# Two token tiles through TensorE's transpose and two through a transposing load, eight W1 units on the first two, an early table load and new issue orders

## The chip, the cores and the metric

The kernel runs on one core of a Trainium2 chip. The metric is device time in microseconds (us) of one execution, as the median of several runs. Profiles come from one execution of their own, and their times count from its first instruction. PE is TensorE, PEld its weight loads, DVE VectorE, ACT ScalarE, POOL GpSimd and SP SyncE; ACTq and SPq are the instruction queues of ACT and SP, which also issue DMAs.

## What is computed

A gated sum of two branches over one input x of 2048 tokens by 512, all bfloat16:

```python
def _A_ref(x, wqkv, w_phi, wo):
    qkv = (x @ wqkv).reshape(B, S, 3, H, Dh).transpose(2, 0, 3, 1, 4)
    q, k, v = qkv[0], qkv[1], qkv[2]
    pq = jnp.einsum("bhsd,hdf->bhsf", q, w_phi)
    pk = jnp.einsum("bhsd,hdf->bhsf", k, w_phi)
    phi_q = jnp.concatenate([_softmax(pq), _softmax(-pq)], axis=-1)
    phi_k = jnp.concatenate([_softmax(pk), _softmax(-pk)], axis=-1)
    kv = jnp.einsum("bhsf,bhsd->bhfd", phi_k, v)
    z  = jnp.einsum("bhsf->bhf", phi_k)
    num = jnp.einsum("bhqf,bhfd->bhqd", phi_q, kv)
    den = jnp.einsum("bhqf,bhf->bhq", phi_q, z)[..., None] + 1e-6
    return (num / den).transpose(0, 2, 1, 3).reshape(B, S, D) @ wo

def _B_ref(x, w1, w2):
    return jnp.maximum(x @ w1, 0) @ w2

g = _sigmoid((x * gate_w).sum(-1, keepdims=True))
return g * _A_ref(x, A_wqkv, A_w_phi, A_wo) + (1 - g) * _B_ref(x, B_w1, B_w2)
```

There are 32 heads of 16, D is 512 and the hidden width of branch B is 1376. Only A_x is read; B_x is not used.

## The kernel before

The kernel is a graph of 622 named tasks. Each has an engine, a function that issues its instructions, and the tasks it depends on. The dictionary ORDER at the top of the file lists, for each of the five engines, the tasks in the order in which that engine issues them; nothing is planned at run time. Waits on semaphores are derived from the dependencies, so an engine stands still at a task until what it depends on is done, and everything behind it in the same list stands too. The `dur`, `lat` and `boost` values in the code belong to the tool that made the lists and have no effect on the chip.

**Tiling.** The tokens are 4 chunks of 512, each of 4 tiles of 128. XT holds x transposed (four row blocks of 128, called j, by tokens), HT the hidden layer, transposed too. PS is the eight banks of PSUM, 512 float32 columns each.

**Names.** A unit `h{chunk}_{k}` is one block of 128 hidden columns (k from 0 to 10) for one chunk: four matmuls of 512 columns, one for each j (`pe_h`, L425), followed by a relu `rl{chunk}_{k}` (L503) into HT. The units 0 to 9 of a chunk use banks 3, 4 and 5 in turn. `f1_{j}` (L408) folds w_phi into the transposed key weights wkT, and `fe1_{j}` evicts the result (L376 on ACT, L378 on DVE). `pr_{k|q}{n}` is the projection of two tiles (L545), `ev_` its eviction (L577), `mx_`/`mn_` the maxima and minima on DVE, `t1_`/`t2_` the subtractions on POOL (L590), `ex_` the exponential on ACT, `sm_`/`rc_` sums and reciprocals on DVE, `nm_` the normalization on POOL (L604, L627). `v{m}` and `ve{m}` are the value projection and its eviction, `kv{m}` (L611) adds a tile to the state. After the last one, `nd{m}` (L654) applies the state to the queries, whose features a transposing DMA `tq{m}` has turned, `o{m}` divides, `to{m}` turns the result, `b{m}` (L676) is the second layer of branch B, `a{m}` (L682) the output projection in the same bank, `oe{m}` (L730) the gated eviction, and `st{m}` the store (L735). The last tile, 15, is cut in two column parts, `a15_0`, `oe15_0`, `st15_0` (ACT's queue, L722) and `a15_1`, `oe15_1`, `st15_1` (SP's queue).

**The first chunk.** x arrives untransposed for its four tiles (`x00` to `x03`, 128 KB each, L306, into spare space of FT), and PE turns each tile by matmuls with an identity (`xt{m}{n}`, L384: two blocks of 128 columns each); `xe{m}{n}` evicts into XT (n 0 on ACT, L396, n 1 on DVE, L399). The other three chunks come by transposing DMAs `x1` to `x3` (L311). W1's columns 0 to 511 come in four row blocks `w1a0` to `w1a3`; columns 512 to 1023 as one load `w1b`, the rest as `w1c`. Units 0 to 3 of chunk 0 are computed piecewise as data comes: `hh00`, `hh01` and `hh1` to `hh4` (`pe_h_first`, L439) take one row block of W1 at a time for all four units on the first 256 tokens, `hr0`, `hr1` units 0 and 1 on the third tile, and `h0_0` to `h0_3` what is left (`pe_h_rest`, L445). Units 4 and up are whole.

At the very start six matmuls on a constant (`warm0`, L292) keep PE busy until x00 is there. The ACT table is loaded by an instruction that the compiler puts in front of the first activation, `xe00`.

These are the heads of the lists around the change, and the end of ACT's:

```python
"sp":  x00 w1a0 w1a2 x02 x03 w1b wphi wkT w1c wv x1 x2 wqT x3 gw w2a w2b wo ...
"act": x01 w1a1 w1a3 xe00 xe10 xe20 xe30 rl0_0 rl0_1 rl0_3 rl0_2 rl0_4 fe1_1 fe1_3 rl0_5 ev_k0 ...
       ... oe10 st9 st10 oe11 st8 st11 oe12 st12 oe13 st13 oe15_0 st15_0
"pe":  warm0 xt00 xt01 xt10 xt11 hh00 hh01 hh1 hh2 xt20 xt21 hh3 xt30 xt31 hh4 hr0 hr1 h0_0 h0_1 h0_2 h0_3
       h0_4 h0_5 f1_0 f1_1 f1_2 f1_3 h0_6 pr_k0a pr_k0 h0_7 h0_8 pr_k1 h0_9 h1_0 ...
```

`x1` waits for `w1c` to have landed; the kernel's last instructions, on SP, wait for all stores.

Of the kernel before, what the change touches and what calls it, by code (L numbers as in the profile page):

```python
# [5 lines left out]
ACT = mybir.ActivationFunctionType  # L6
# [12 lines left out]
        "x00 w1a0 w1a2 x02 x03 w1b wphi wkT w1c wv x1 x2 wqT x3 gw w2a w2b wo hx0 hx1 hx2 tq0 tq1 "  # L19
        "hx3 to0 tq2 tq3 to1 tq4 tq5 to2 to3 tq6 to4 tq7 to5 tq8 to6 tq9 to7 tq10 tq11 to8 to9 tq12 "  # L20
        "to10 tq13 tq14 to11 tq15 to12 to13 to14 to15 st14 st15_1 "
    ),
    "pool": (
        "iota_r iota_i iota_c ones hpad t1_k0 t2_k0 t1_k1 t2_k1 t2_k2 t1_k2 t1_k3 t2_k3 nm_k0 nm_k1 t1_k5 t1_k4 t2_k4 "
        "nm_k2 nm_k3 t1_k6 t1_k7 t2_k7 t2_k5 nm_k4 t1_k8 t2_k6 t2_k8 nm_k5 t2_q0 t1_q0 nm_k6 t2_q1 t1_q1 nm_k7 "
        "ra_q0 nm_q0 nm_k8 t2_q2 t1_q2 ra_q1 nm_q1 t1_q3 t2_q3 ra_q2 nm_q2 t1_q4 t2_q4 ra_q3 nm_q3 t1_q5 t2_q5 "
        "ra_q4 nm_q4 t2_q6 t1_q6 ra_q5 nm_q5 t2_q7 t1_q7 t2_q8 t1_q8 ra_q6 nm_q6 ra_q7 nm_q7 ra_q8 nm_q8 "
    ),
    "act": (
        "x01 w1a1 w1a3 xe00 xe10 xe20 xe30 rl0_0 rl0_1 rl0_3 rl0_2 rl0_4 fe1_1 fe1_3 rl0_5 ev_k0 rl0_8 rl0_6 "  # L30
        "rl0_7 ev_k1 rl1_0 rl0_9 ev_k2 rl1_1 ex_k0 ev_k3 rl1_3 rl1_2 ve0 rl1_5 ex_k1 rl1_4 ve1 ev_k4 rl1_6 rl1_7 "
        "ex_k3 rl1_8 ev_k5 ex_k2 ve2 rl0_10 rl1_9 ev_k6 rl1_10 ve3 rl2_0 rl2_1 ve4 ex_k4 rl2_2 ev_k7 rl2_3 rl2_4 "
        "ve5 rl2_6 rl2_5 rl2_7 ve6 rl2_8 rl2_9 rl2_10 ve7 ex_k5 ev_k8 ge1 ve8 ge0 ex_k7 rl3_0 rl3_1 ve9 ev_q0 "
        "ex_k6 ve10 gp0 ev_q1 rl3_3 ex_k8 gp1 rl3_2 rl3_4 ve11 ev_q2 ex_q0 rl3_5 ve12 ev_q3 ve13 rl3_6 ve14 ev_q4 "
        "rl3_7 ex_q1 rl3_8 ve15 rl3_9 rl3_10 ex_q2 ev_q5 ex_q3 ev_q6 oe0 ev_q7 ex_q4 oe1 st1 oe2 st0 ex_q5 "
        "ge3 ev_q8 oe3 oe4 st3 oe5 ge2 st2 ex_q6 gp2 oe6 ex_q7 st5 st4 ex_q8 st6 oe7 oe8 gp3 oe9 st7 oe10 st9 st10 "
        "oe11 st8 st11 oe12 st12 oe13 st13 oe15_0 st15_0 "
    ),
    "dve": (
        "ident shift xe01 xe11 xe21 xe31 blk row4 wbd1 wbd3 mk wbd2 wbd0 fe1_0 fe1_2 mx_k0 mn_k0 mx_k1 mn_k1 "  # L40
        "mn_k2 mx_k2 mx_k3 mn_k3 sm_k0 rc_k0 sm_k1 rc_k1 mn_k4 mx_k4 mx_k5 sm_k2 gr0 rc_k2 gr1 mx_k6 sm_k3 rc_k3 "
        "mn_k7 sm_k4 mx_k7 rc_k4 mn_k5 gr2 fe0_0 fe0_1 fe0_2 fe0_3 mn_k6 mx_k8 mn_k8 sm_k5 rc_k5 mn_q0 mx_q0 "
        "sm_k6 rc_k6 sm_k8 go1 go0 sm_k7 mn_q1 mx_q1 rc_k7 sm_q0 mx_q2 rc_q0 rc_k8 mx_q3 mn_q3 mn_q2 mx_q4 sm_q1 "
        "kn1 kn0 kz0 kz1 rc_q1 mn_q4 gr3 rd0_1 rd0_0 o0_0 o0_1 sm_q2 rd1_0 rd1_1 rc_q2 mx_q5 o1_1 o1_0 mn_q5 "
        "rd2_0 rd2_1 o2_0 o2_1 sm_q3 rd3_1 rd3_0 rc_q3 o3_1 o3_0 mn_q6 rd4_1 o4_1 rd4_0 o4_0 sm_q4 rd5_0 rd5_1 "
        "rc_q4 o5_0 o5_1 mx_q6 rd6_1 rd6_0 o6_1 o6_0 sm_q5 rd7_1 rc_q5 o7_1 rd7_0 mx_q7 o7_0 mx_q8 mn_q8 mn_q7 "
        "rd8_0 rd8_1 o8_0 o8_1 sm_q6 rd9_1 rd9_0 rc_q6 o9_0 o9_1 rd10_1 rd10_0 o10_0 sm_q7 go2 o10_1 sm_q8 rd11_1 "
        "rd11_0 o11_0 rc_q8 o11_1 rc_q7 rd12_0 rd12_1 o12_1 o12_0 rd13_0 go3 rd13_1 o13_1 o13_0 rd14_0 rd14_1 "
        "o14_0 o14_1 rd15_0 rd15_1 o15_0 o15_1 oe14 oe15_1 "
    ),  # L50
    "pe": (
        "warm0 xt00 xt01 xt10 xt11 hh00 hh01 hh1 hh2 xt20 xt21 hh3 xt30 xt31 hh4 hr0 hr1 h0_0 h0_1 h0_2 h0_3 h0_4 "
        "h0_5 f1_0 f1_1 f1_2 f1_3 h0_6 pr_k0a pr_k0 h0_7 h0_8 pr_k1 h0_9 h1_0 pr_k2 h1_1 h1_2 pr_k3 h1_3 v0 h1_4 h1_5 v1 "
        "h1_6 pr_k4 h1_7 h1_8 v2 pr_k5 h1_9 kv0 h0_10 kv1 pr_k6 h1_10 v3 kv2 h2_0 h2_1 kv3 v4 pr_k7 h2_2 v5 h2_3 "
        "h2_4 h2_5 h2_6 h2_7 v6 h2_8 h2_9 h2_10 kv4 kv5 f0_0 kv6 f0_1 v7 f0_2 pr_k8 f0_3 h3_0 kv7 h3_1 v8 pr_q0 "
        "v9 h3_2 h3_3 v10 kv8 pr_q1 kv9 h3_4 v11 kv10 pr_q2 h3_5 kv11 v12 pr_q3 h3_6 v13 kv12 h3_7 v14 kv13 pr_q4 "
        "h3_8 h3_9 v15 kv14 h3_10 pr_q5 kv15 b0 nd0_0 nd0_1 b3 nd1_0 nd1_1 b2 pr_q6 a0 nd2_0 nd2_1 b1 nd3_1 pr_q7 "
        "nd3_0 b4 nd4_1 nd4_0 a1 pr_q8 nd5_1 a2 nd5_0 b5 a3 nd6_0 nd6_1 b6 nd7_0 nd7_1 a4 a5 b7 nd8_1 nd8_0 a6 b9 "
        "nd9_0 nd9_1 b8 nd10_0 nd10_1 a7 b10 nd11_1 a8 nd11_0 a9 b11 a10 nd12_0 nd12_1 b13 nd13_1 nd13_0 b12 "
        "nd14_0 nd14_1 b14 nd15_0 nd15_1 a11 a12 a13 b15_0 a14 a15_0 b15_1 a15_1 "  # L60
# [122 lines left out]
def bass_gated_mix__linear_kernel_hedgehog__dense_activation_relu__prompt_kernel(  # L183
# [38 lines left out]
    with ExitStack() as es:  # L222
# [101 lines left out]
        def load_w(j, eng, lat):  # L324
            load(f"w1a{j}", eng, W1[:, j, 0:512], w1r[:, j, 0:512], dur=0.45, lat=lat)
# [3 lines left out]
        load_w(0, "sp", 3.2)  # L329
        load_w(1, "act", 3.4)  # L330
        load_w(2, "sp", 3.8)
        load_w(3, "act", 3.95)
        load_x(2, "sp", 4.0)
        load_x(3, "sp", 3.9)
        load("w1b", "sp", W1[:, :, 512:1024], w1r[:, :, 512:1024], dur=0.5, lat=5.0)
        load("wphi", "sp", WPS[:, :, :], A_w_phi.rearrange("(g hl) r c -> (hl r) g c", g=ND), dur=0.5, lat=4.9)
        load_t("wkT", WT[:, ND:2 * ND, :], A_wqkv[:, D:2 * D], (), 4.1, 2.7)
# [42 lines left out]
        XB, FB = ((0, 1), (6, 7), (0, 1), (6, 7)), (0, 1, 6, 7)  # L380
# [7 lines left out]
        for m in range(4):  # L388
            for n in range(2):
                add(f"xt{m}{n}", "pe", lambda q, m=m, n=n: pe_xt(q, m, n),  # L390
                    (f"x0{m}", "ident", f"xe{m - 2}{n}" if m > 1 else None), dur=0.2, boost=9000.0 - 10 * m)
            for n, eng in enumerate(("act", "dve")):
                xo = XT[:, 2 * n:2 * n + 2, m * P:(m + 1) * P]
                xi = PS[:, XB[m][n], 0:2 * P].rearrange("p (j t) -> p j t", j=2)
                if eng == "act":
                    add(f"xe{m}{n}", eng, lambda q, o=xo, i=xi: q.activation(o, i, ACT.Copy), (f"xt{m}{n}",), dur=0.35,  # L396
                        boost=9000.0 - 10 * m)
                else:
                    add(f"xe{m}{n}", eng, lambda q, o=xo, i=xi: q.tensor_copy(o, i), (f"xt{m}{n}",), dur=0.37,  # L399
                        boost=9000.0 - 10 * m)  # L400
        x0 = [f"xe{m}{n}" for m in range(4) for n in range(2)]
# [11 lines left out]
        for c in range(NC):  # L413
            units += [("h", c, k) for k in range(KT - 1)]
# [5 lines left out]
        freed[FB[2]] = ("xe30",)  # L420
        w1of = {k: (() if k < 4 else ("w1b",) if k < 8 else ("w1c",)) for k in range(KT)}
# [15 lines left out]
        def pe_h_first(q, j, c0, c1, ks=range(4)):  # L437
            for k in ks:
                last = q.matmul(PS[:, GB4[k], c0:c1], W1[:, j, k * P:(k + 1) * P], XT[:, j, c0:c1],  # L439
# [3 lines left out]
        def pe_h_rest(q, k, c0, c1, first):  # L443
            for j in range(ND):
                last = q.matmul(PS[:, GB4[k], c0:c1], W1[:, j, k * P:(k + 1) * P], XT[:, j, c0:c1],  # L445
                                start=(j == 0 and first), stop=(j == ND - 1), skip_group_check=True)
            return last


        GB4 = (*HB, 2)  # L450
# [3 lines left out]
        for n, (j, ks) in enumerate(((1, range(4)), (2, range(4)), (3, (0, 1)), (3, (2, 3)))):  # L454
            add(f"hh{n + 1}", "pe", lambda q, j=j, ks=ks: pe_h_first(q, j, 0, 2 * P, ks),
                (f"xe0{j // 2}", f"xe1{j // 2}", f"w1a{j}", prev), dur=0.11 * len(ks), boost=8500.0)
            prev = f"hh{n + 1}"

        for k in range(2):
            add(f"hr{k}", "pe", lambda q, k=k: pe_h_rest(q, k, 2 * P, 3 * P, True), ("xe20", "xe21", prev), dur=0.22,  # L460
                boost=8200.0)
            prev = f"hr{k}"
        for line in (("warm0", "xt00", "xt01", "xt10", "xt11", "hh00", "hh01", "hh1", "hh2", "xt20", "xt21", "hh3", "xt30", "xt31",
                      "hh4", "hr0", "hr1"), ("xe00", "xe10", "xe20", "xe30"),
                     ("ident", "shift", "xe01", "xe11", "xe21", "xe31", "blk", "row4", "mk")):
# [10 lines left out]
        for n, (kind, a, k) in enumerate(units):  # L476
            b = GB4[n] if n < 4 else FB[2] if n == 4 else HB[(n - 4) % len(HB)]
            if kind == "h":
                halved = n < 4
                deps = [*xof[a], *w1of[k], prev, *freed[b]]  # L480
                if k == KT - 1:
# [17 lines left out]
                    pe_h_rest(q, k, (3 if k < 2 else 2) * P, 4 * P, k > 1) if h else pe_h(q, a, k, b),  # L499
                    deps, dur=(0.22 if k < 2 else 0.44) if halved else 0.87,  # L500
# [279 lines left out]
```

## Time and profile before

| | us |
|---|---|
| median of 3 runs | 150.24 (150.15 to 150.57) |
| the profiled execution | 149.87 |
| its span, first to last instruction | 148.3 |
| PE busy | 145.5 |
| DVE busy | 111.7 |
| POOL busy | 109.6 |
| ACT busy | 91.4 |

An engine's busy time is the sum of the stretches in which it executes; matmuls overlap each other, since the next starts before the one ahead has left the array. A line of the chain or of the timeline gives the start, the length, the engine (and in the chain what it writes), the line of the code and the number of instructions merged; brackets give the idle time ahead and what ended it. The first microseconds of the other engines, from the timeline:

```profile
3.99 0.81 ACT L396 ACTIVATE XT<-PS 128x256 bf16<-128x256 f32 x2 [0.56 <-PE PS L384]
4.20 0.85 DVE L399 CAST XT<-PS 128x256 bf16<-128x256 f32 x2 [1.84 <-PE PS L384]
...
6.55 0.82 ACT L396 ACTIVATE XT<-PS 128x256 bf16<-128x256 f32 x2 [1.75 <-PE PS L384]
...
6.67 0.87 DVE L399 CAST XT<-PS 128x256 bf16<-128x256 f32 x2 [1.61 <-PE PS L384]
```

### The profile page before, as it was taken

How to read it: one execution, taken by the hardware profiler on the slowest of the kernel's cores; microseconds unless marked ns; L12 is line 12 of the kernel's file. 1: busy time of each engine (PE TensorE's matmuls, PEld its weight loads, DVE VectorE, ACT ScalarE, POOL GpSimd, SP SyncE). 2: the span in 40 equal slices, each digit the busy share in tenths (PEclk: the TensorE clock that was granted, in tenths of full speed). 3: DMA queues.
4: the chain of work that ended last, by engine and by line, in shares of the span. 5: the costliest groups of instructions: out<-in, count | busy, mean ns of one | idle time of the engine just before them, and what ended most of it. 6: DMA issues, size and time to landing. Idle time of an engine off the chain costs nothing.

```text
span 148.3 us, 2542 instructions
## 1 busy us (share of the span) xinstructions
PE 145.5 (98%) x1009; PEld 75.3 (51%) x1009; DVE 111.7 (75%) x169; ACT 91.4 (62%) x126; POOL 109.6 (74%) x72
## 2 busy tenths in 40 slices
PE   7999999999999999999999999999999999999994
PEld 2875444445654475445444545455444444445453
DVE  2433666998896948989999997999999988634502
ACT  3475769799969765898983937175583751310141
POOL 4000499999999999999999999999999793150000
PEclk9999999999999999999999999999999999999999
DMA  4998999910040001000000093646957785556752
GB/s 139 324 256 220 169 187 214 340 51 4 0 73 0 0 4 38 0 0 4 0 0 0 7 141 71 141 95 138 183 119 167 180 214 116 141 134 158 64 157 92
DMA packets 46363, 16.11 MB, mean 109 GB/s; under 512 B 39856, under 2 KB 46352, under 8 KB 46352
## 3 DMA queue, kind: packets, MB, share of 16 engines
q1 hardware_dynamic: 43760, 13.61, 42.6%
q10 hardware_dynamic: 2592, 2.34, 4.9%
q8 instruction: 8, 0.13, 0.4%
q14 instruction: 3, 0.02, 0.1%
HBM read 4.41 MB, written 2.10 MB: 44 GB/s over the span
## 4 chain that ended last, share of the span: by engine, by line
PE 98%; DVE 0%; issue 0%
PE PS L676 24%; PE PS L425 21%; PE PS L545 19%; PE PS L526 9%; PE PS L682 9%; PE PS L611 3%; PE PS L654 3%; PE PS L433 2%; PE PS L292 2%; PE PS L698 2%; PE PS L439 2%; PE PS L445 1%; PE PS L408 1%; PE PS L384 1%; PE PS L709 1%; DVE OSB L719 0%
## 5 line engine op out<-in xcount | busy, mean ns | idle before, releaser
L590 POOL TENSOR_TENSOR TS<-PB,MX 128x1024 bf16<-128x1024 bf16 (+1 forms) x18 | 30.9, 1723 | 14.5 <-DVE MX L581 14.5
L676 PE MATMUL PS<-W,HT 128*128 128x512 bf16 (+1 forms) x165 | 38.1, 379 | 0.0
L597 DVE TENSOR_REDUCE ZB<-FT 128x128 f32<-128x2048 bf16 (+1 forms) x18 | 36.6, 2031 | 1.8 <-ACT FT L595 1.8
L595 ACT ACTIVATE FT<-TS 128x2048 bf16<-128x2048 bf16 (+1 forms) x18 | 30.9, 1718 | 9.6 <-POOL TS L590 9.5
L425 PE MATMUL PS<-XT,W 128*128 128x512 bf16 x144 | 34.7, 379 | 0.0
L590 POOL TENSOR_TENSOR TS<-MN,PB 128x1024 bf16<-128x1024 bf16 (+1 forms) x18 | 30.9, 1726 | 0.8 <-DVE MN L583 0.8
L545 PE MATMUL PS<-WP,XT 128*128 128x512 bf16 x128 | 30.6, 379 | 0.0
L604 POOL TENSOR_TENSOR FT<-FT,SC 128x2048 bf16<-128x2048 bf16 (+1 forms) x9 | 29.6, 3293 | 0.0
L503 ACT ACTIVATE HT<-PS 128x512 bf16<-128x512 f32 x40 | 22.6, 597 | 5.4 <-PE PS L425 4.6
L581 DVE TENSOR_REDUCE MX<-PB 128x64 bf16<-128x1024 bf16 (+1 forms) x18 | 19.5, 1085 | 5.9 <-ACT PB L577 5.9
L676 PEld LDWEIGHTS PS<-W,HT 128*128 128x128 bf16 (+1 forms) x165 | 15.4, 98 | 16.9
L730 ACT ACTIVATE OSB<-PS,OMG 128x512 bf16<-128x512 f32 x14 | 9.6, 686 | 21.1 <-PE PS L682 20.5
L583 DVE TENSOR_REDUCE MN<-PB 128x64 bf16<-128x1024 bf16 (+1 forms) x18 | 19.3, 1084 | 3.2 <-ACT PB L577 3.2
L425 PEld LDWEIGHTS PS<-XT,W 128*128 128x128 bf16 x144 | 13.7, 98 | 15.4
L577 ACT ACTIVATE PB<-PS 128x1024 bf16<-128x1024 f32 (+1 forms) x18 | 16.7, 927 | 7.2 <-PE PS L545 4.0
L545 PEld LDWEIGHTS PS<-WP,XT 128*128 128x128 bf16 x128 | 12.1, 98 | 13.5
L526 PE MATMUL PS<-WV,XT 128*128 128x512 bf16 x64 | 16.4, 379 | 0.0
L627 POOL TENSOR_TENSOR FT<-FT,SR 128x1024 bf16<-128x1024 bf16 (+1 forms) x9 | 15.7, 1740 | 0.7
L682 PE MATMUL PS<-WO,OT 128*128 128x512 bf16 x60 | 14.9, 378 | 0.0
L663 DVE SCALAR_TENSOR_TENSOR OTM<-PS,EG,RD 128x256 bf16<-128x256 f32 x32 | 13.8, 463 | 0.2
L661 DVE RECIPROCAL RD<-PS 128x16 f32<-128x16 f32 x32 | 6.4, 232 | 9.0 <-PE PS L654 8.8
L535 ACT ACTIVATE VS<-PS 128x512 bf16<-128x512 f32 x16 | 9.6, 602 | 4.3 <-PE PS L526 4.3
(55 smaller groups left out, 106.6 us busy)
## 6 DMA issues: line engine op xcount, KB each, us to landing
out_dram<-OSB ACTq DMA_DIRECT2D x14, 128.0 KB, 2.2
W<-in_B_w_dram SPq DMA_DIRECT2D x1, 1280.0 KB, 7.5
W<-in_B_w_dram SPq DMA_DIRECT2D x1, 512.0 KB, 4.5
WV<-in_A_wqkv_dram SPq DMA_DIRECT2D x1, 512.0 KB, 4.9
WO<-in_A_wo_dram SPq DMA_DIRECT2D x1, 512.0 KB, 7.5
FT<-in_A_x_dram SPq DMA_DIRECT2D x3, 128.0 KB, 3.1
W<-in_B_w_dram SPq DMA_DIRECT2D x1, 352.0 KB, 4.1
W<-in_B_w_dram ACTq DMA_DIRECT2D x2, 128.0 KB, 3.3
```

What stands on the lines that cost most here:

```text
L425: last = q.matmul(PS[:, b, :], W1[:, j, k * P:(k + 1) * P], XT[:, j, chunk(c)], start=(j == 0), stop=(j == ND - 1))
L503: add(f"rl{a}_{k}", "act", lambda q, a=a, k=k, b=b: q.activation(HT[:, k, chunk(a)], PS[:, b, :], ACT.Relu), (prev,), dur=0.6, boost=RL)
L526: last = q.matmul(PS[:, 2, :], XT[:, j, m * P:(m + 1) * P], WV[:, j, :], start=(j == 0), stop=(j == ND - 1))
L545: last = q.matmul(PS[:, n, :], XT[:, j, m * P:(m + 1) * P], WP[:, s, j, :], start=(j == 0), stop=(j == ND - 1))
L581: add(f"mx_{J}", "dve", lambda q, sl=sl, w=w, i=pbg: q.tensor_reduce(MX[:, sl, 0:w * H], i, AX.X, ALU.max), (f"ev_{J}", old("t1")), dur=0. ...
L583: add(f"mn_{J}", "dve", lambda q, sl=sl, w=w, i=pbg: q.tensor_reduce(MN[:, sl, 0:w * H], i, AX.X, ALU.min), (f"ev_{J}", old("t2")), dur=0. ...
L590: add(f"{tn}_{J}", "pool", lambda q, o3=o3, a3=a3, b3=b3: q.tensor_tensor(o3, a3, b3, ALU.subtract), (f"{'mx' if sg == 0 else 'mn'}_{J}", ...
L595: add(f"ex_{J}", "act", lambda q, fs=fs, ts=ts, w=w: q.activation(FT[:, fs, 0:w * F], TS[:, ts, 0:w * F], ACT.Exp), (f"t1_{J}", f"t2_{J}", ...
L597: add(f"sm_{J}", "dve", lambda q, fs=fs, sl=sl, w=w: q.tensor_reduce(ZB[:, sl, 0:2 * w * H], FT[:, fs, 0:w * F].rearrange("p (g d) -> p g ...
L604: add(f"nm_{J}", "pool", lambda q, f3=f3, sl=sl, w=w: q.tensor_tensor(f3, f3, SC[:, sl, 0:2 * w * H].unsqueeze(2).to_broadcast([P, 2 * w * ...
L676: last = q.matmul(PS[:, ab, :], HT[0:r, k, m * P:(m + 1) * P], W2[0:r, k, :], start=(k == 0), stop=False)
L682: last = q.matmul(PS[:, ab, :], OT[:, m % NOT, t, :], WO[:, t, :], start=False, stop=(t == ND - 1))
```

## The change

Tiles 2 and 3 of the first chunk no longer go through PE: `x02`, `x03`, `xt20` to `xt31` and `xe20` to `xe31` are gone, and one transposing DMA `x0b` writes their part of XT, behind `wphi` and ahead of `wkT` on SP. W1's columns 512 to 1023 come in four row blocks `w1b0` to `w1b3`, two on SP and two on ACT. Units 4 to 7 of chunk 0 get the treatment of units 0 to 3: `hg0` to `hg3` take one row block each for the four of them on the first 256 tokens, in banks 0, 1, 6 and 7, and all eight units have their other 256 tokens done later, units 4 to 7 first. Three of the eight relus move to DVE. A new activation `first` of one column, behind `x01` on ACT, makes the table load come there. All lists but POOL's are written anew.

```diff
     "sp": (
-        "x00 w1a0 w1a2 x02 x03 w1b wphi wkT w1c wv x1 x2 wqT x3 gw ...
+        "x00 w1a0 w1a2 w1b0 w1b2 wphi x0b wkT w1c wv x1 x2 wqT x3 gw ...
     "act": (
-        "x01 w1a1 w1a3 xe00 xe10 xe20 xe30 rl0_0 rl0_1 rl0_3 rl0_2 rl0_4 fe1_1 fe1_3 rl0_5 ev_k0 ...
-        "oe11 st8 st11 oe12 st12 oe13 st13 oe15_0 st15_0 "
+        "x01 first w1a1 w1a3 w1b1 w1b3 xe00 xe10 rl0_4 rl0_6 fe1_1 fe1_3 rl0_2 ev_k0 rl0_0 rl0_9 rl0_3 ev_k1 ...
+        "oe3 oe4 st1 st3 ev_q8 oe5 ex_q6 oe6 ex_q7 oe7 ex_q8 st4 st5 st7 oe9 oe8 st8 st9 st6 oe10 oe11 oe12 st11 "
+        "st10 oe13 st12 oe15_0 st15_0 st13 "
     "dve": (
-        "ident shift xe01 xe11 xe21 xe31 blk row4 wbd1 wbd3 mk wbd2 wbd0 fe1_0 fe1_2 mx_k0 mn_k0 ...
+        "ident shift xe01 xe11 blk row4 wbd1 wbd3 mk wbd2 wbd0 rl0_5 rl0_7 fe1_0 fe1_2 rl0_1 mx_k0 mn_k0 ...
     "pe": (
-        "warm0 xt00 xt01 xt10 xt11 hh00 hh01 hh1 hh2 xt20 xt21 hh3 xt30 xt31 hh4 hr0 hr1 h0_0 h0_1 h0_2 h0_3 h0_4 "
-        "h0_5 f1_0 f1_1 f1_2 f1_3 h0_6 pr_k0a pr_k0 h0_7 h0_8 pr_k1 h0_9 h1_0 pr_k2 ...
-        "... v15 kv14 h3_10 pr_q5 kv15 b0 nd0_0 nd0_1 b3 ...
+        "warm0 xt00 xt01 xt10 xt11 hh00 hh01 hh1 hh2 hh3 hg0 hg1 hg2 hg3 h0_4 h0_5 h0_6 h0_7 h0_0 f1_0 f1_1 f1_2 "
+        "f1_3 h0_1 h0_2 pr_k0a pr_k0 h0_3 h0_8 h0_9 pr_k1 h1_0 v0 pr_k2 ...
+        "... v15 kv14 h3_9 pr_q5 h3_10 kv15 b0 nd0_0 nd0_1 b3 ...
...
-        load_x(2, "sp", 4.0)
-        load_x(3, "sp", 3.9)
-        load("w1b", "sp", W1[:, :, 512:1024], w1r[:, :, 512:1024], dur=0.5, lat=5.0)
+        add("first", "act", lambda q: q.activation(EP[:, 0:1], bass.AP(tensor=one, offset=0, ap=[[1, P], [1, 1]]), ACT.Copy),
+            (), dur=1.5)
+        after_last("first", "act")
+        for part, n in (("a", 0), ("b", 512)):
+            for j in range(ND):
+                load_w(part, n, j, ("sp", "act")[j % 2], 3.3)
         load("wphi", "sp", ...)
+        load_t("x0b", XT[:, :, 2 * P:4 * P], x2[2 * P:4 * P, :], (), 1.3, 2.5)
         load_t("wkT", ...)
...
-        for m in range(4):
+        for m in range(2):
...
-        x0 = [f"xe{m}{n}" for m in range(4) for n in range(2)]
+        x0 = [*(f"xe{m}{n}" for m in range(2) for n in range(2)), "x0b"]
...
+        GB8 = (*HB, 2, *FB)
+        for j in range(ND):
+            add(f"hg{j}", "pe", lambda q, j=j: pe_h_first(q, j, 0, 2 * P, range(4, 8)),
+                ("xe00", "xe01", "xe10", "xe11", f"w1b{j}", prev), dur=0.44, boost=8500.0)
+            prev = f"hg{j}"
...
-                    pe_h_rest(q, k, (3 if k < 2 else 2) * P, 4 * P, k > 1) if h else pe_h(q, a, k, b),
+                    pe_h_rest(q, k, 2 * P, 4 * P) if h else pe_h(q, a, k, b),
...
+                if a == 0 and k in (1, 5, 7):
+                    add(f"rl{a}_{k}", "dve", lambda q, a=a, k=k, b=b: q.tensor_scalar(
+                        HT[:, k, chunk(a)], PS[:, b, :], 0.0, None, ALU.max), (prev,), dur=0.69, boost=RL)
+                else:
+                    add(f"rl{a}_{k}", "act", ...)
...
-            war = [f"xe{2 + j // 2}{j % 2}"] + (["rl0_4"] if j == 2 else [])
+            war = [f"rl0_{4 + j}"]
             add(f"f1_{j}", "pe", lambda q, j=j, b=b: pe_fold(q, 1, j, b), ("wkT", *wbd, *war), ...)
```

## The prediction

> **What bounds the kernel now.** I read the page's busy table first, then the chain of waits in order of time, then the timeline of the first microseconds and of the last ones, then the waits.
>
> ```profile
> span 148.3 us, 2542 instructions
> ...
> PE 145.5 (98%) x1009; PEld 75.3 (51%) x1009; DVE 111.7 (75%) x169; ACT 91.4 (62%) x126; POOL 109.6 (74%) x72
> ...
> PE 98%; DVE 0%; issue 0%
> ```
>
> The chain never leaves TensorE. From 20.00 to 146.40 the busy times by stretch show 126.36 us of 126.40, so PE runs without a hole and the span is the time to its first full-rate matmul, plus its work, plus the tail behind its last one. In the chain, 8 pieces carry the early part:
>
> ```profile
> 3.58 1.01 PE PS L384 x8
> 4.59 1.81 PE PS L439 x16
> 6.41 0.22 PE PS L384 x4
> 6.63 0.22 PE PS L439 x2
> 6.85 0.22 PE PS L384 x4
> 7.07 0.22 PE PS L439 x2
> 7.29 1.88 PE PS L445 x24
> 9.16 1.73 PE PS L425 x8
> ```
>
> L384 is the transpose of x by matmul, 128 columns each. The first eight take 1.01/8 = 0.126 us apiece, the next two groups 0.22/4 = 0.055. So PE runs at half rate at first; single starts in the trace put the step near 5.5 us (128 columns every 0.107 us before, 256 every 0.109 after). The granted-clock row reads 9 throughout and doesn't show this.
>
> ```profile
> 2.15 1.28 ACT L396 ACT_TABLE_LOAD   x1 [2.15 <-issue]
> ...
> 3.58 1.01 PE L384 MATMUL PS<-IDN,FT 128*128 128x128 bf16 x8
> ...
> 4.11 3.27 SPq L311 DMA_TRANSPOSE WT<-in_A_wqkv_dram  x1
> ...
> 119.21 1.06 ACT L595 ACTIVATE FT<-TS 128x1024 bf16<-128x1024 bf16 x1 [0.75 <-POOL TS L590]
> 119.22 0.85 ACTq L735 DMA_DIRECT2D out_dram<-OSB  x2
> ...
> 146.40 0.34 ACTq L722 DMA_DIRECT2D out_dram<-OSB  x1
> 146.40 0.32 DVE L719 TENSOR_SCALAR OSB<-PS,OMG 128x96 bf16<-128x96 f32 x1 [0.59 <-PE PS L709]
> 146.75 0.35 SPq L722 DMA_DIRECT2D out_dram<-OSB  x1
> ```
>
> At 119.22 two DMAs are issued while ACT still computes what stands ahead of them: ACT's queue does not hold a DMA behind a running activation. The last line is the store that ends the span, landing 1.5 us later at 148.29; the one at 146.40 lands at 148.11.
>
> **Removed work.** xt20 to xt31 leave: the two "0.22 PE PS L384 x4" pieces, **-0.44 us** of PE. With them goes a wait of PE for xe21 and xe31: L445's first matmul starts 0.22 after its forerunner of 256 columns, which needs 0.11, so **-0.11**. The four evictions of these tiles (0.82 on ACT, 0.87 on DVE) hid behind PE's work and give nothing.
>
> **Split work.** Units 4 to 7 are now two matmuls of 256 columns instead of one of 512: 2 x 0.109 against 0.216, 16 times, +0.04; units 0 and 1 lose their 128-column halves (2 x 0.056 against 0.109, 8 times), -0.02. Together +0.02.
>
> **First products.** Until hh1 PE does the same as now. hh1 starts at 5.26 (0.55, the clock steps in it), hh2 and hh3 take 0.44 each, hg0 to hg3 0.44 each: hg0 starts at 6.68, hg3 at 7.99, done at 8.43. The four blocks w1b0 to w1b3 take the places of x02 and x03 on SP and follow w1a3 on ACT. Now the 128 KB loads land one behind the other at 4.12, 4.33, 4.83, 5.10, 5.37 and 5.68, some 0.3 apart, so the four land at about 5.4, 5.7, 6.0 and 6.3 (estimate). Cover 1.3 us or more; cost 0.
>
> **Table load moved up.** `first` puts the 1.28 us of the table load and an activation (0.2, the 128x4 ones) behind x01, ahead of four DMA issues. Left where it was, it would start after five issues (0.41 and 4 x 0.46) at 3.05, end at 4.33, and delay xe00 (3.99 now) by 0.34; moved up, it ends at 2.5. The trace shows no issue behind a table load. Bounds: 0 if the queue runs on as at 119.22, 1.28 on w1a1 if it holds. In the second case w1a1 is issued at about 2.5 and lands 2.9 to 3.2 later, 5.4 to 5.7, where hh1 wants it at 5.26: 0.15 to 0.45. I take 0, by the row at 119.22.
>
> **x0b.** It stands behind wphi on SP, issued at 3.08 + 0.55 = 3.63. It is 1024 packets of 256 bytes; wkT's 2048 took the DMA engines from 6.5 to 8.9, in full flow 1,130 a microsecond, and landed 0.6 later. The engines now have 1.25 MB ahead of it, not 1.5, and wphi's small packets (0.5): free at about 6.1, x0b through at 7.0, landed at 7.6. h0_4 asks at 8.43: **cover 0.8, cost 0**. The far bound is x1's row, 5.7 us from issue to landing: 9.3, a stall of 0.87. I take 0 because x1's own packets had run by 15.1 and waited for a 16 KB instruction fetch that began at 15.24 and took 0.96. Behind h0_4 on PE stands everything.
>
> **What x0b pushes back on SP.** wkT's packets end at about 9.1 instead of 8.9 (256 KB of plain load less, 0.64; 1024 packets more, 0.91), it lands near 9.75, and f1_0 asks at 8.43 + 4 x 0.437 + 0.437 = 10.61. w1c, wv and x1 (which waits for w1c) shift by as much: x1 17.23 to about 17.5. h1_0 now comes earlier: 10.61 + f1 0.89 + h0_1, h0_2 0.87 + pr_k0 1.73 + h0_3 0.44 + h0_8, h0_9 1.73 + pr_k1 1.73 = 18.0. Cover 0.5; cost 0. x2, wqT and x3 have many microseconds.
>
> **Relu on DVE.** Three of 128x512 at 0.65 to 0.7 (L378's casts, 1.29 for two). DVE idles 2.3 and 3.0 us around fe1 now. rl0_7 would run 10.35 to 11.05, f1_3 asks at 11.28. Cost 0; with the cover gone, up to 0.5.
>
> **New orders.** POOL's list is the same. Its L590 starts at 16.77 and it has no hole until 116.3; what starts it is pr_k0, ending at 14.21 now and at 14.10 after. So POOL gains 0.11 where PE gains 0.53. nm_k8 ends at 86.04, kv15 starts at 86.50 and would come to 85.97: the 0.46 of slack goes, and I put **+0.08** for the hand-over. At b0 and nd the trace's slack is 0.5 to 1.3, at a0 to a15 over 1.1; I found no other new wait when I walked the lists with these durations.
>
> **Tail.** In ACT's list st13 moved behind st15_0, which waits for oe15_0, the last but one result. Two issues in a row start 0.37 apart (119.22 and 119.59): st13 goes out at 146.40 + 0.37 = 146.77 on today's scale and, at 1.7 us for 128 KB (st13 and st14 now), lands at 148.47 to 148.5, against 148.29 for st15_1. **+0.2**. Bounds: 0 (landing like st15_1, 1.5), and +1.0 by the slower of the pair at 119.22, 2.5 us, which shared the engines with transposes that are over here.
>
> **Sum.** -0.44 - 0.11 + 0.02 + 0.08 + 0.2 = **-0.25 us**. The profiled execution took 149.87 (span 148.3), so 149.62 on its scale; the median of the runs is 150.24, so **150.0**. What a measurement of this kernel tells from no change is about 0.3%, 0.45 us: the forecast is no measurable change, on the fast side.
>
> **Rivals.**
> *A, the tail is free and the cut counts more* (0.22). If st13 lands with st15_1, -0.45 is left. In executions slower than the profiled one (150.15 to 150.57 against 149.87) the clock may step later, and transposes removed at half rate are worth 0.107 x 8 = 0.86: about -0.6. Time 149.65. Against it: st13's place in the list.
> *B, x0b is late* (0.18, slower). Its place is h0_4. It costs nothing until it lands after 8.43 and turns the change slower by over 0.3% from about 9.15 on. At x1's pace, 9.3: -0.25 + 0.87 = +0.6; a late wkT behind it adds some. Time 150.9. For it: every DMA transpose of 512 rows took 4.9 to 6.2 us to land. Against: half the rows, and the engines' rate.
> *C, POOL's chain takes the bound* (0.09). If ev_k0 or mx_k0 comes 0.4 later than I reckon, kv15 waits for nm_k8 and the whole 0.53 is lost; with the tail 150.45. For: rc_k0 has 0.38 in hand before nm_k0.
> *D, the table load holds ACT's queue* (0.07). hh1 waits 0.15 to 0.45: 150.35. It would also mean the change doesn't do what it says: an earlier table and later weights.
>
> *E, the clock steps later* (0.06). Now it steps some 4.7 us after PE's first matmul (0.77). Each microsecond by which the step comes later costs 0.5 us of PE; 1.2 later makes +0.35 of -0.25: 150.6, half of it over the bound. For: the runs shown spread from 149.87 to 150.57 with one and the same program. Against: up to hh1, where the step falls, PE's work is unchanged.
>
> The Trainium skill's page "TensorE: Matmul & The Clock Gate", Part 1, says that the window which watches TensorE's activity runs freely, so that one kernel can show different numbers of slow matmuls from run to run. That speaks for E, and for its mirror inside A; the trace shows one step only.
>
> **How the numbers follow.** The forecast has 0.38. It is faster by over 0.45 us one time in five, else within. A: faster 0.85. B: slower 0.9. C: slower 0.4. D: slower 0.35. E: slower 0.5. With A 0.22, B 0.18, C 0.09, D 0.07 and E 0.06: faster 0.08 + 0.19 = 0.27; slower 0.16 + 0.04 + 0.02 + 0.03 = 0.25; same 0.48. The range runs from A's time less its run-to-run 0.2 to short of B's, 149.4 to 150.8.
>
> **What would show it.** In the new profile: no L384 after the first eight; the first projection (L545 now) near 12.4 instead of 12.5, with no idle in front of h0_4 (a wait for the XT transpose there is B); W1 issues on ACT from 1.2 on during the table load (from 2.5 on is D); kv15 following its forerunner (a wait for POOL is C); PE's end near 145.9; and st13 as the last or last but one landing, some 2.1 us behind PE's end. If PE ends at 145.9 and the time doesn't fall, the tail is mis-sized; if PE ends at 146.4 again, one of the covers was.

## The result, and the profile after

The changed kernel takes **151.45 us** (median of 6 runs, 151.12 to 151.78), the kernel before 150.20 in runs beside them (6 runs, 149.92 to 150.57). The ratio is 1.0079 [1.0059, 1.0099]: slower by 1.2 us, where 150.0 was forecast, and outside the forecast range. The profiled execution of the changed kernel took 151.41, its span is 150.1. One profile further down, the first with an earlier instruction fetch, is of an execution that was 1.5 us late from its first microseconds on; no line of it is used.

The page of the changed kernel: span, the busy times, the chain by engine, and the one group of matmuls with a wait of its own.

```profile
span 150.1 us, 2523 instructions
...
PE 144.8 (96%) x991; PEld 76.4 (51%) x1009; DVE 113.1 (75%) x170; ACT 88.6 (59%) x122; POOL 109.6 (73%) x72
...
PE 94%; DMA 3%; issue 1%; DVE 0%
...
L684 PE MATMUL PS<-WO,OT 128*128 128x512 bf16 x56 | 14.1, 378 | 1.3 <-DMA OT<-OTM 1.2
```

Before, the chain was 98% PE. Now 3% of it is a DMA, and the output projections (L684) have stood 1.2 us for the transposing DMA from OTM to OT. (The 1% "issue" are pieces of some 0.05 us: 991 of 1009 matmuls have a record.) The chain of the changed kernel, in order of time (start, length, what), shows the front and the place of the wait:

```profile
3.51 1.01 PE PS L384 x8
4.52 4.66 PE PS L438 x36
9.18 2.18 PE PS L444 x20
11.36 0.89 PE PS L408 x16
12.26 0.87 PE PS L444 x8
...
121.44 0.96 PE PS L678 x5
122.39 4.98 DMA OT<-OTM
127.37 0.27 issue
127.65 0.81 PE PS L684 x3
```

L384 comes once, for eight transposes; the other pieces of it are gone. At 122.39 `to9` is issued, the transposing DMA of tile 9's result. It lands 4.98 us later, at 127.37, and `a9`, its output projection, waits for it with everything behind it on PE. From the completion times of PE's tasks, each less its forerunner's and less its work, two tasks of the changed kernel come late after 11 us: `a9` by 1.15 and `kv15` by 0.14. Before there is none.

Two lists changed here; the diff shown with the change has of this only ACT's new order:

```diff
     "pe": (
-        "nd9_0 nd9_1 b8 nd10_0 nd10_1 a7 b10 nd11_1 a8 nd11_0 a9 b11 a10 ...
+        "nd9_0 nd9_1 a6 b8 nd10_1 nd10_0 b10 a9 nd11_1 nd11_0 b11 a8 ...
     "act": (
-        "... oe5 ge2 st2 ex_q6 gp2 oe6 ex_q7 st5 st4 ex_q8 st6 oe7 oe8 gp3 oe9 st7 ...
+        "... oe5 ex_q6 oe6 ex_q7 oe7 ex_q8 st4 st5 st7 oe9 oe8 st8 st9 ...
```

`a9` now stands ahead of `a8`, and three stores that went out elsewhere follow `ex_q8`. In the kernel before, PE asked for `a9` at 127.20, 2.9 us after `to9` had landed (124.28); now it asks at 126.29. The timeline of the changed kernel (start, length, engine, what) at the start, there, and at the end:

```profile
1.18 1.28 ACT L329 ACT_TABLE_LOAD   x1 [1.18 <-PEq L767]
...
1.24 1.36 ACTq L306 DMA_DIRECT2D W<-in_B_w_dram  x3
...
121.00 3.48 SPq L670 DMA_TRANSPOSE OT<-OTM  x2
...
122.41 0.84 ACTq L737 DMA_DIRECT2D out_dram<-OSB  x2
...
123.71 0.73 ACTq L737 DMA_DIRECT2D out_dram<-OSB  x1
...
148.09 0.36 SPq L724 DMA_DIRECT2D out_dram<-OSB  x1
148.11 0.45 ACTq L737 DMA_DIRECT2D out_dram<-OSB  x1
```

`st4` leaves 0.02 us after `to9` is issued (the line with OT merges `to8` and `to9`), `st5` 0.4 us and `st7` 1.3 us after it. The DMA answers for the two stretches add a third companion. First the changed kernel from 122.38 to 126.50, by queue (packets, MB, share) and by issue (KB, us to landing):

```profile
q1 hardware_dynamic: 1000, 0.25, 67.3%
q10 hardware_dynamic: 420, 0.39, 53.9%
q8 instruction: 1, 0.02, 1.4%
...
out_dram<-OSB ACTq DMA_DIRECT2D x3, 128.0 KB, 3.7
OT<-OTM SPq DMA_TRANSPOSE x1, 5.0
```

and the kernel before from 121.90 to 124.30, all of `to9`'s way:

```profile
q1 hardware_dynamic: 546, 0.13, 24.7%
q10 hardware_dynamic: 144, 0.13, 16.7%
...
OT<-OTM SPq DMA_TRANSPOSE x1, 2.4
```

In the timeline of the kernel before, this line merges `to8` and `to9`:

```profile
119.23 3.87 SPq L668 DMA_TRANSPOSE OT<-OTM  x2
```

Before, `to9` had one store beside it (144 packets of ACT's queue q10) and took 2.4 us. Now it has three, and a fetch of 16 KB of instructions (q8, one packet, 123.08 to 124.01), and takes 5.0. The kernel before also fetches, from 121.58 to 122.61, and issues `to9` 0.33 after the fetch has begun: the rest of the fetch, 0.70 us, falls into `to9`'s way, and it still takes 2.4. There the fetch began in the way of `to8` (issued 119.23, landed 123.71), which took 4.48 us. `to9` also stands closer behind `to8` now, 1.39 us instead of 2.68. That is not the reason: in the kernel before, `to13` is issued 1.31 behind `to12` with no store and no fetch beside it, and takes 2.43.

So the time goes like this, against the forecast's PE end of 145.93 on the profile's scale: `a9` 1.15, the front 0.59 (`f1_0` done at 11.60 instead of 11.01), `kv15` 0.06 more than taken; together 147.73, and PE's end is 147.72. (11.01 is the end of `f1_0` before, 11.13, less the 0.55 of removed work, plus the 0.43 by which more of the units now stands ahead of it.) Behind it `st13` lands last, 0.32 behind `st15_1`, instead of 0.2.

### The profile page after: what moved, and what is told of

Same layout as the page of the kernel before. It is cut to its first block, busy times and chain, and to the rows that moved or that the text cites. A ratio compares the mean times of both kernels' runs of the same rounds, so it can differ in the third digit from the quotient of the medians.

```text
span 150.1 us, 2523 instructions
## 1 busy us (share of the span) xinstructions
PE 144.8 (96%) x991; PEld 76.4 (51%) x1009; DVE 113.1 (75%) x170; ACT 88.6 (59%) x122; POOL 109.6 (73%) x72
## 4 chain that ended last, share of the span: by engine, by line
PE 94%; DMA 3%; issue 1%; DVE 0%
PE PS L678 21%; PE PS L547 18%; PE PS L424 18%; PE PS L528 9%; PE PS L684 8%; DMA OT<-OTM 3%; PE PS L438 3%; PE PS L613 3%; PE PS L656 3%; PE PS L444 2%; PE PS L432 2%; PE PS L292 2%; PE PS L700 2%; PE PS L408 1%; PE PS L384 1%
## 5 line engine op out<-in xcount | busy, mean ns | idle before, releaser
L424 PE MATMUL PS<-XT,W 128*128 128x512 bf16 x124 | 30.7, 379 | 0.2
L547 PE MATMUL PS<-WP,XT 128*128 128x512 bf16 x124 | 29.9, 379 | 0.3
L505 ACT ACTIVATE HT<-PS 128x512 bf16<-128x512 f32 x37 | 21.4, 598 | 9.1 <-PE PS L444 5.4
L424 PEld LDWEIGHTS PS<-XT,W 128*128 128x128 bf16 x128 | 12.1, 98 | 13.5
L684 PE MATMUL PS<-WO,OT 128*128 128x512 bf16 x56 | 14.1, 378 | 1.3 <-DMA OT<-OTM 1.2
```

What stands on the lines that cost most here:

```text
L424: last = q.matmul(PS[:, b, :], W1[:, j, k * P:(k + 1) * P], XT[:, j, chunk(c)], start=(j == 0), stop=(j == ND - 1))
L505: add(f"rl{a}_{k}", "act", lambda q, a=a, k=k, b=b: q.activation(HT[:, k, chunk(a)], PS[:, b, :], ACT.Relu), (prev,), dur=0.6, boost=RL)
L547: last = q.matmul(PS[:, n, :], XT[:, j, m * P:(m + 1) * P], WP[:, s, j, :], start=(j == 0), stop=(j == ND - 1))
L684: last = q.matmul(PS[:, ab, :], OT[:, m % NOT, t, :], WO[:, t, :], start=False, stop=(t == ND - 1))
```

## The experiments

All changes are to the changed kernel unless it says otherwise. Differences to it are taken between ratios to the kernel before, 1% being 1.5 us. The question was which of `a9`'s wait, the front and the tail made the 1.2 us, and what makes `to9` late.

**a9 behind a8 again.** From `a8` on, PE's list and the evictions on ACT are put in the order of the tiles:

```diff
-  "... b10 a9 nd11_1 nd11_0 b11 a8 nd12_0 nd12_1 b13 a10 nd13_0 nd13_1 b12 "
+  "... b10 a8 nd11_1 nd11_0 b11 a9 nd12_0 nd12_1 b12 a10 nd13_0 nd13_1 b13 "
-  "... st4 st5 st7 oe9 oe8 st8 st9 ..."
+  "... st4 st5 st7 oe8 oe9 st8 st9 ..."
```

> The changed kernel with a8 ahead of b11 and a9 behind it (and b12 ahead of b13, oe8 ahead of oe9). In the changed kernel PE stands at a9 from 126.3 to 127.6, waiting for to9, which lands at 127.37. Theory 'a9 came too early for to9': a9 is then asked for at about 129.1, to9 is there, the 1.3 us go and nothing takes their place: 151.4 - 1.2 = 150.2. Rival 'late transposes will hit whatever stands there': a8 waits for to8 or the wait turns up at b12, 151.0 or more.

Measured: 149.91 us (12 runs), ratio to before 0.9990 [0.9974, 1.0006]. Against the changed kernel that is 0.0089, 1.3 us (0.9 to 1.7), and `a9`'s 1.15 lies in it. The chain of this kernel at the place:

```profile
124.16 2.38 PE PS L678 x11
126.53 0.06 issue
126.59 0.81 PE PS L684 x3
127.40 0.25 PE PS L656 x8
127.65 2.38 PE PS L678 x11
130.03 0.87 PE PS L684 x4
```

No DMA is left in it, though `to9` is as slow as before (issued 122.48, landed 127.51, 5.0 us): `a9` now asks at 130.03, `a8` at 126.59, whose own transpose landed at 125.57. The delay of `to9` costs nothing unless `a9` asks early.

**The stores earlier.**

```diff
-  "... oe5 ex_q6 oe6 ex_q7 oe7 ex_q8 st4 st5 st7 oe9 oe8 ..."
+  "... oe5 ex_q6 st4 st5 oe6 ex_q7 oe7 ex_q8 oe9 st7 oe8 ..."
```

> The changed kernel with the stores st4 and st5 issued behind ex_q6 (about 115.6) and st7 behind oe9, so that ACT issues no store between 121 and 128; a9 stays where it is. Theory 'the three stores in a row hold up to9': to9 lands some 2.4 us after its issue as in the kernel before (124.28 for 121.91), so by about 125, and a9 doesn't wait: 150.2. Rival 'the instruction fetch at 123.08 (16 KB, 0.93 us) holds it up': to9 still lands after 126.5 and 151.0 or more remains.

Measured: 150.25 us, ratio 1.0008 [0.9995, 1.0021], 1.1 us less than the changed kernel. PE's order is that of the changed kernel, and `a9` doesn't wait. The DMA answer from 122.20 to 125.80:

```profile
q1 hardware_dynamic: 1024, 0.25, 106.8%
q8 instruction: 1, 0.02, 1.6%
...
OT<-OTM SPq DMA_TRANSPOSE x1, 3.5
```

ACT's queue q10 is gone from the stretch, the instruction fetch is still in it, and `to9` takes 3.5 us instead of 5.0: below what `a9` has in hand.

**The instruction fetch earlier.** Six warm-up matmuls of 512 columns become 24 of 128, the same time on PE; PE's later instructions move on by 18 matmuls and their weight loads, so its fetches come sooner.

```diff
-    WARM = (6 * (512,),)
+    WARM = (24 * (128,),)
```

> The changed kernel with the six warming matmuls of 512 columns cut into 24 of 128: the same 2.6 us of PE, but 36 more instructions in PE's stream, so that every later instruction fetch comes 18 matmuls, some 3.5 us, sooner (the one at 123.08 near 119.5). Theory 'the fetch holds up to9': to9 lands by about 125.5, a9 doesn't wait, 150.2, unless to8 or tq11 is hit in its place. Rival 'the stores do': to9 still after 126.5, about 151.4.

Measured: 150.37 us, ratio 1.0012 [0.9993, 1.0031]. What `to9` does is read from a second series of the same kernel:

> The kernel of e3_fetch_early once more, whose profile fell into an execution about 1.5 us late from its start, so that its to9 can't be read. Theory 'the fetch and the stores each cost to9 about 1 us, and only both together are more than a9 can spare': the fetch comes near 121, before to9's issue, to9 lands about 3 us after its issue, a9 waits 0.3 or less, 150.4. Rival 'the fetch has no part in it': to9 takes 4.5 us or more again and a9 waits 0.8 or more; then 150.4 needs another reason.

Measured: 150.89 us, ratio 1.0050 [1.0028, 1.0073]. The fetch comes at 119.0, ahead of `to9`, and the chain has:

```profile
121.56 1.98 PE PS L678 x10
123.54 3.09 DMA OT<-OTM
126.62 0.05 issue
126.67 1.04 PE PS L684 x4
```

With the three stores beside it and no fetch, `to9` lands 3.09 us after its issue, but was issued at 123.54 instead of 122.39: the fetch now fell into the turn of a transpose ahead of it on SP, whose issue took 2.4 us. `a9` waits 0.28 instead of 1.15. The two series stand at 1.0 us and, beside the changed kernel in the same session, 0.6 us under it (0.0 to 1.2 for the second); both below it, their size uncertain: one and the same kernel gave 1.0012 and 1.0050, each outside the other's interval, so a difference of half a microsecond between two series is not safe.

**The tail.** `st13` ahead of the last tile's result on ACT:

```diff
-  "st10 oe13 st12 oe15_0 st15_0 st13 "
+  "st10 oe13 st12 st13 oe15_0 st15_0 "
```

> The changed kernel with st13 ahead of oe15_0 in ACT's list. Now st13 lands at 149.93, 0.3 behind st15_1 at 149.61 and 0.5 behind st15_0. Theory 'st13 is the tail': the last landing is st15_1 or st15_0 again, -0.3 us, 151.1. Rival 'the stores at the end share the engines and st13 is covered': st13 lands early and the others no sooner, or the next store takes its place; no change, 151.4.

Measured: 150.77 us, ratio 1.0039 [1.0025, 1.0052], 0.2 to 1.0 us under the changed kernel. `st13` lands at 145.21 and `st15_1` ends the span. The tail's 0.3 is in the interval, near its lower end. In this profile `a9` waited 0.82 instead of 1.15, since `to9` took 4.66 instead of 4.98 (its issue and PE's request both came 0.6 earlier). That and the tail would make 0.6, but whether `a9` waits less in every execution of this kernel isn't shown. The mirror image says more: the kernel **before**, with `st13` put last.

```diff
-  "oe11 st8 st11 oe12 st12 oe13 st13 oe15_0 st15_0 "
+  "oe11 st8 st11 oe12 st12 oe13 oe15_0 st15_0 st13 "
```

> The kernel before with st13 moved behind st15_0 on ACT and nothing else. Theory 'st13 behind st15_0 is the tail': it lands 0.2 to 0.35 behind what now lands last, 150.2 + 0.3 = 150.5. Rival 'it shares the last microsecond with the other stores and nothing is seen': 150.2.

Measured: 150.33 us, ratio 1.0019 [1.0001, 1.0037], +0.3 us. Its timeline:

```profile
6.60 0.40 PE L384 MATMUL PS<-IDN,FT 128*128 128x128 bf16 x4 [0.55 <-DMA FT<-in_A_x_dram]
...
146.77 0.34 ACTq L722 DMA_DIRECT2D out_dram<-OSB  x1
...
147.12 0.36 SPq L722 DMA_DIRECT2D out_dram<-OSB  x1
147.14 0.45 ACTq L735 DMA_DIRECT2D out_dram<-OSB  x1
```

`st13` is issued 0.02 behind `st15_1` and lands at 148.96, 0.27 after it (148.69). The first line shows something else: in this execution the kernel before, whose front is untouched, waits 0.55 for x's third tile, which its first profile didn't.

**Both mended.** `a8` ahead of `a9` (with `oe8 st7 oe9` on ACT), `st4 st5` behind `ex_q6`, `st13` ahead of `oe15_0`; the front as changed.

> The changed kernel with the three order edits together: a9 behind b11, st4 and st5 behind ex_q6 and st7 behind oe8, st13 ahead of oe15_0. Theory 'the new front is worth about what was forecast and the loss sits in the lists of the last third': e1's 149.9 less the 0.3 of the tail, 149.6, faster than the kernel before (150.2) by 0.4 to 0.6. Rival 'the front gives nothing, since its loads land about 1 us late': no better than 150.1.

Measured: 149.80 us, ratio 0.9978 [0.9963, 0.9993]. `to9` takes 3.6 us, `st13` lands early, `kv15` is the one late task (0.13). This front with these repairs is faster than the kernel before by 0.3 us.

**The table load left where it was.** The kernel just above without `first`:

```diff
-        add("first", "act", lambda q: q.activation(EP[:, 0:1], ...
-        after_last("first", "act")
-        "x01 first w1a1 w1a3 w1b1 w1b3 xe00 ...
+        "x01 w1a1 w1a3 w1b1 w1b3 xe00 ...
```

> The kernel of e5_mended without the activation first, so that the table load stands behind five DMA issues on ACT. Theory 'the early table load is needed with five issues': the load runs from 3.05 to 4.33 and xe00 starts there instead of at 3.9 to 4.0, so everything on PE comes 0.3 to 0.4 later: e5 + 0.35. Rival 'the first products wait for W1 and the clock anyway': the delay is swallowed in front of hh2, 0 to 0.1.

Measured: **149.64 us**, ratio 0.9971 [0.9955, 0.9987], and not the 0.35 more that was expected: it beats both kernels, though it can't be told from the one with `first`. Its timeline shows that the early load does what it says, all the same:

```profile
3.11 1.28 ACT L393 ACT_TABLE_LOAD   x1 [3.11 <-issue]
...
4.84 3.88 PE L435 MATMUL PS<-XT,W 128*128 128x128 bf16 x36 [0.33 <-ACT XT L393]
```

Without `first` the load sits at 3.11, the first eviction starts at 4.41 (3.87 with it), and PE waits 0.33 for it. No difference in the time is left that 12 runs can tell; the traces don't settle why.

**The front's loads.** The kernel **before** with W1's second part in four blocks, two of them on ACT, and `first`:

```diff
-        "x00 w1a0 w1a2 x02 x03 w1b wphi ...
+        "x00 w1a0 w1a2 x02 x03 w1b0 w1b2 wphi ...
-        "x01 w1a1 w1a3 xe00 ...
+        "x01 first w1a1 w1a3 w1b1 w1b3 xe00 ...
```

> The kernel before with only W1's second 512 columns split into the four row blocks of the changed kernel, two of them on ACT, and with first; x02 and x03 stay, and there is no x0b. In the five profiles of the changed front w1a2 lands at 5.5 to 6.1 and w1a3 at 5.7 to 6.6, against 4.83 and 5.10 before. Theory 'loads on both queues share the engines, and those behind slow those ahead': w1a2 and w1a3 land after 5.4 here too. Rival 'it is the transposing load x0b, issued at 3.55': they land at 4.8 to 5.2 as before. Time: 150.2 to 150.6.

Measured: 150.67 us, ratio 1.0041 [1.0022, 1.0059]. Its timeline has a wait for W1's third block, which lands at 5.82 (4.83 in the profile of before, 4.90 in the other profile of that front):

```profile
5.96 0.60 PE L443 MATMUL PS<-XT,W 128*128 128x256 bf16 x4 [0.30 <-DMA W<-in_B_w_dram]
```

There is no `x0b` in this kernel, so `x0b` isn't what makes the block late.

Two more divide the loads otherwise, on the best kernel (without `first`): one load of 512 KB on SP,

```diff
-        "x00 w1a0 w1a2 w1b0 w1b2 wphi ...
+        "x00 w1a0 w1a2 w1b wphi ...
-        "x01 w1a1 w1a3 w1b1 w1b3 xe00 ...
+        "x01 w1a1 w1a3 xe00 ...
```

> The mended kernel without first (e6, 149.6) with W1's second 512 columns as one load on SP, as in the kernel before; hg0 to hg3 all wait for it. Theory 'loads on ACT's queue delay w1a2 and w1a3 by sharing the engines': these land by about 5.0, hh2 doesn't wait; hg0 is asked for at 6.7 to 7.3 and w1b lands at 7.0 to 7.5; about -0.1 to -0.2 where the clock steps early, 149.5. Rival 'it is single slow packets of the engines, whoever queues': w1a2 or w1a3 late by up to 1 us again, and hg0 now waits for the whole of w1b: 149.8 to 150.0.

Measured: 150.14 us, ratio 0.9997 [0.9977, 1.0017]. The third block lands at 6.02, the whole second part at 7.53, and `hg0` waits for it (the unit ahead is done at 7.26). No second block stands on ACT's queue here, so that queue isn't the reason either. The other has four blocks, all on SP:

```diff
-        "x00 w1a0 w1a2 w1b0 w1b2 wphi ...
+        "x00 w1a0 w1a2 w1b0 w1b1 w1b2 w1b3 wphi ...
-        "x01 w1a1 w1a3 w1b1 w1b3 xe00 ...
+        "x01 w1a1 w1a3 xe00 ...
```

> The mended kernel without first (e6, 149.6) with the four blocks w1b0 to w1b3 all on SP, behind w1a2, and none on ACT. Theory 'the queues' sharing delays w1a2 and w1a3': they land by about 5.0, and the blocks behind them one by one as before, 149.5. Rival 'single slow packets': w1a2 or w1a3 late again; x0b is issued 0.95 later, lands near 9.3 and h0_4 waits for it some 0.3 to 0.5: 149.9.

Measured: 149.73 us, ratio 0.9977 [0.9959, 0.9994], like the best kernel. The third block lands at 4.97, but `x0b`, two issues further back on SP, lands no earlier (8.71), and here it is what PE waits for:

```profile
8.76 2.36 PE L441 MATMUL PS<-XT,W 128*128 128x256 bf16 x20 [0.44 <-DMA XT<-in_A_x_dram]
```

Over all these profiles, the third block's landing sorts by what is issued within 0.05 us of 2.13 beside it: 128 KB (before, before with `st13` last, all four blocks on SP) 4.83 to 4.97; 256 KB (the fronts with a block on either queue) 5.42 to 6.13; 512 KB 6.02. That speaks for a shared way, but the fourth block doesn't sort so: 5.10, 5.53 and 6.33 with 128 KB, 5.72 to 6.64 with 256. In each profile 6 to 32 single packets of 1 KB take 0.25 to 1.2 us (others 0.046). Whether they carry the delay isn't shown, and what makes them slow stays open.

**The changed kernel once more**, beside the last three:

> The changed kernel once more, unchanged, for a second profile of it and its time beside the edited ones. Theory 'a9's wait for to9 is there in every execution': PE stands again 0.8 to 1.5 us at a9, to9 landing more than 3.5 us after its issue, 151.0 to 151.5. Rival 'it was one bad profile': no wait at a9, and the time has another cause.

Measured: 151.56 us (6 runs), ratio 1.0090 [1.0059, 1.0121]; `to9` again 5.0 us, `a9` late by 1.14, `kv15` by 0.16. The wait is the kernel's, not one execution's.

What `to9` takes from issue to landing, over all these profiles:

| beside it | us |
|---|---|
| mostly one store; a fetch that began 0.07 to 0.33 ahead of the issue (before, and its two variants) | 2.4 to 2.5 |
| three stores, no fetch | 3.1 |
| a fetch that began 0.6 to 0.8 behind the issue, no store | 3.5 to 3.6 |
| three stores and such a fetch | 4.7 to 5.0 |

The rows are `to9`'s alone. `to8`, into whose way the fetch began 2.0 to 2.6 us behind its issue, took 4.4 to 4.6 with stores and without; in the second series with the earlier fetch, which has none there, it took 3.25 beside the stores.

## Why the prediction was wrong, step by step

**The step that failed** is "New orders": "at a0 to a15 over 1.1; I found no other new wait when I walked the lists with these durations." The term put there is 0; it measured 1.15. With before's 2.4 us for `to9`, `a9` would indeed have had a cushion of 1.5 (it asks at 126.3; 122.4 and 2.4 make 124.8), so the list was read rightly. The duration was wrong: `to9` was given the time that it had with its old neighbours, while the same diff moved three stores next to it and the shift of PE's work a fetch. Each alone adds 0.7 to 1.2, less than the cushion; together they add 2.6. The prediction had evidence of both kinds in hand: a store of the pair at 119.22, at 2.5 us, that shared the engines with transposes, which it used for the tail alone, and `x1`'s wait for a 16 KB instruction fetch, which it used for `x0b` alone. The profile of before also had the rows for tiles like this one: 2.98 and 3.12 us beside two stores (`to4`, `to11`), 3.56 with a fetch and part of a store (`to3`), 4.21 and 4.48 with both (`to14`, `to8`). With `to8`'s 4.48 `to9` would land at 126.9, and `a9` would wait 0.6. Moving `a9` (1.3 us back) or the stores (1.1 back) removes the loss; that taking the stores away is enough, with the fetch still there, fits a cushion that only their sum exceeds. The fetch's part rests on the rows of `to9` and on one profile without a fetch there, in which `a9` still waits 0.28; its worth to the time is uncertain. Added to the forecast, 150.0 and 1.3 come to 151.3, where 151.45 was measured.

**The rest of the sum came out about right.** With `a9`'s wait removed and the tail as it is, the changed kernel is 0.15 us under before (interval -0.4 to +0.1); -0.25 was forecast. With the tail mended too it is 0.3 under; -0.45 was rival A's sum. What each of its parts is worth alone, the transposes above all, was not measured, and luck may have a share: the first fold was reckoned to start at 10.6, and starts at 10.61 to 11.29 in the seven profiles with this front, at 10.73 and 11.10 in the two of before's.

**Tail.** Right, a little small: +0.27 in the kernel before, +0.32 in the changed profile, against +0.2. `st13` goes out 0.37 behind `st15_0`, as reckoned, but its landing takes 1.8 us instead of 1.7, with `st15_1` on the engines at the same time.

**POOL's hand-over.** `kv15` is late by 0.13 to 0.16 in every profile with this front, against 0.08. Rival C's place was right, its price wasn't.

**Table load.** Rival D is refuted: of the four W1 issues on ACT, at 1.24, 1.66, 2.14 and 2.63, three start during the load from 1.18 to 2.46. The first eviction was reckoned 0.34 late without `first`; it came 0.54 behind that of the kernel with it and PE stood 0.33. Its worth to the time was not seen.

**First products and x0b.** The costs of 0 held in the changed profile to about 0.1 us, the landings didn't: W1's third block came at 6.02, and `hh2` started at 6.15 instead of 6.03 (in the profile with the stores moved PE idles 0.39 there); `w1b0` to `w1b3` at 6.75 to 7.65 (5.4 to 6.3 estimated), `x0b` at 8.71 (7.6). They were reckoned from the one profile of before, in which W1's third block landed at 4.83, where the same kind of front with more beside it has 5.4 to 6.1. The cover of 0.8 ahead of `h0_4` shrank to 0 to 0.5, and where the clock steps early or `x0b` is issued later, PE stands there by up to 0.44. So rival B had the right place, in other runs than this one, and half its price.

**The clock.** The front's 0.59 in the changed profile is rival E's mechanism: PE works at half rate (128 columns in 0.107 us, 256 in 0.213) up to 6.7 there, up to 5.5 before, and 1.2 us at half rate are 0.6 of work. It need not belong to the change: in the other profiles of this front and its variants the step lies between 3.9 and 6.8, a wider spread than the difference. In the second profile of before's front it came at 4.8, and PE then ran into the wait of 0.55 shown above: an earlier step can be given back at the next load. The spread agrees with the rule of the Trainium skill's page "TensorE: Matmul & The Clock Gate", Part 1, that the window runs freely and the number of slow matmuls differs from run to run.

Of the signs named beforehand, the transposes, the issues on ACT and `st13` came as said; the first projection came near 12.97 instead of 12.4 (the clock; its first matmul has no record, the ones ahead start 0.109 apart up to 12.86), and PE's end at 147.72 instead of 145.9. "If PE ends at 146.4 again, one of the covers was" mis-sized pointed the right way: a cover was, by 2.6 us, though not one of those that the prediction listed.

## What to carry to other kernels

When a new order moves transfers, a transfer that stands still in the list gets new neighbours: reckon its landing anew with every DMA that is issued within its flight on any queue, the instruction fetches too, and hold the cushion of the consumer against the slowest row of that kind of transfer (here `to8`'s 4.48 us, in the profile of before), not against its own old row. Where one execution's loads give a cover of less than a microsecond, take a late landing into the range. A cushion that survives either of two delays can fall to both, so undoing one of them shows that it matters, not that it alone does.

## What was not expected of the hardware

A transposing DMA of one 128-token tile took 2.3 to 2.4 us by itself. `to9` took 3.1 with three stores of 128 KB issued beside it, 3.5 to 3.6 with a 16 KB instruction fetch that began behind its issue, and 4.7 to 5.0 with both. A fetch that had begun 0.07 to 0.33 us ahead of the issue and ran on for 0.70 to 0.89 us left it at 2.4 to 2.5, with one store beside it. During the changed kernel's `to9` the DMA engines together moved at most 20 GB/s from 123.5 to 124.7, and 317 on average in the microsecond from 124.8 on. The packets that were under way just before the fetch, the last of `to8` (started from 122.76 to 123.06), took 1.8 to 2.0 us, where others take about 0.05; with the stores moved away they did so too (1.7 to 2.0), so the hold doesn't need the stores. In most executions `to9`'s issue also took 2.0 to 2.1 us instead of 1.2 to 1.3 when a fetch began in it; in one it took 1.22 and the landing was nearly as late (4.7), so the long issue isn't the cause. What holds the packets stays open.

The Trainium skill's page "Runtime: NRT & Kernel Launch", section "Instruction fetch mechanics", calls the cost of crossing a 16 KiB block of instructions mostly hidden. For PE's own stream the trace of before agrees: from 20.00 to 146.40 it has seven such fetches, and PE is busy for 126.36 of the 126.40 us. A transposing DMA into whose way a fetch began landed some 1.1 us later all the same, and with `a9` behind it the time showed it.

DMA issues on ACT's queue went on during a table load, 0.42 to 0.49 us apart, against 0.44 and 0.49 without it.
